# Linear attention and a two-expert MoE in one launch: gate weights loaded inside a batch's v, planned costs changed, a 96-row rest tile and new ranks

## The chip, the cores and the metric

The kernel runs on 1 core of one Trainium2 chip, in one launch. The metric is the device time in microseconds (us) of that launch.

## The reference

Linear attention over 8 batches (8 heads, 576 positions, head size 64), then a mixture of experts (MoE) on its 4608 output rows of 512:

```python
q_s = softmax(q, axis=-1)                    # over the head's 64
k_s = softmax(k, axis=2)                     # over the 576 positions
kv  = einsum('bhsd,bhse->bhde', k_s, v)
attn = einsum('bhsd,bhde->bhse', q_s, kv)
x   = attn.transpose(0, 2, 1, 3).reshape(4608, 512)
logits = x @ w_gate + modality_bias[modality_id]       # 8 experts
e = argmax(logits);  gate = softmax(logits)[e]
out[row] = gate * (relu(x[row] @ w1[e]) @ w2[e])       # w1 512x1024, w2 1024x512
```

With this draw the bias decides the expert, so all rows of modality 0 (2277 of them) go to one expert and all of modality 1 (2331) to another.

## The kernel before

**Work.** For each batch b, q, k and v come by DMA from SyncE's queue into five staging buffers `st` (two halves of a transfer for b = 0 to 2, one transfer after that). ScalarE takes the exponentials of q and k. VectorE sums q per head (`sq`, L883), and takes the reciprocal (`iq`, L894 and L895). GpSimd multiplies q by it (`nq`, L899, five steps). TensorE transposes and sorts q by modality with a permutation matrix (`s1`, L1101; the matrix is `perm`, L928, on VectorE), builds kv (`kv`, L1014), and VectorE normalizes it (`ki`, L1041 and L1044; `kb`, L1050). TensorE then multiplies the two (`s2`, L1140), and ScalarE and VectorE copy the columns to their places in `xs` (`put`, L1171): rows of modality 0 from the left ("side a"), of modality 1 from the right ("side b").

**Places.** They come from the modality ids: `isa`, `turn`, `isa2`, `rank`, `pos`, `off` and `aoff` count; `slot`, `digits`, `hhi`, `hv`, `hlo`, `id` and `idx` make the list of row numbers for the stores; `bsel` (GpSimd, L727 to L732) gives each row its bias.

**Experts.** The two experts' weights come by GpSimd's queue into `W` (`wi`, L537 and L548): a1 and a2 are w1 and w2 of side a, b1 and b2 those of side b, each in two pieces. GpSimd needs the experts' numbers for this (`eid`). The first, a1, also awaits the second half of q1. The gate weights (`lwg`, L478, four small DMAs of SyncE's queue; `wgc`, L609, their cast on VectorE) are needed by the logits. Each side works off nine passes of 256 rows: logits (L1217), `gates`, h = relu(x w1) (L1289 on TensorE; L1251 and L1253 the relu on ScalarE or VectorE), y = h w2 (L1302), scaling (L1257, L1259) and one indirect store for each 128 rows (L1262, GpSimd). The boundary between the two modalities lies within one more tile, the rest (`ffn_rest`), whose expert is chosen at run time: `copy_x`, a copy of the weights, h (L1455), y (L1468) and a store.

**Order.** Nothing of the order is written by hand. `Plan.order` simulates the kernel with assumed costs: every engine, when idle in the plan, starts the ready step with the least priority, and the order that comes out is the order of each engine's real queue, which is served strictly in order. A step's priority is its `rank` plus the first number that `TUNED` has for its key; the second number is added on VectorE and GpSimd where a step may go to more than one engine. `Plan.later` holds a step back until another is done, in the plan alone. DMA loads keep the order of `transfers`. `Plan.fill` puts matmuls that nobody reads (`unread`, L1556) into TensorE's planned idle time up to `quiet`, at which one PSUM buffer more joins the ring.

```python
self.prio = {e: rank + more + (late if ALONE[e] and len(costs) > 1 else 0.0) for e in costs}
```

After the plan a few steps test that all the assumptions on the draw hold (counts per batch, one expert for each modality); only where they don't, a slow loop at the end runs.

Of the kernel before, what the change touches and what calls it, by code (L numbers as in the profile page):

```python
# [19 lines left out]
P = 128  # L20
# [224 lines left out]
def kernel(  # L245
# [27 lines left out]
    GW = 256  # L273

    passes_a = [(n, 256 * n, 256) for n in range(B)] + [(B - 1, 256 * B, 256)]
    passes_b = [(n, N - lo - w, w) for n, lo, w in passes_a]
    W2 = KD * F
    WSZ = KD * F + KF * D
    OOB = 9000.0

    pool = ctx.enter_context(tc.tile_pool(name="all", bufs=1))
    psum = ctx.enter_context(tc.tile_pool(name="ps", bufs=1, space=bass.MemoryType.PSUM))

    def sb(shape, dtype, name):
        return pool.tile(shape, dtype, name=name)
# [94 lines left out]
    def hlo(c, n):  # L380
# [26 lines left out]
    bulk = [x for x in transfers if x != "g"]  # L407
    ahead_of = {(y[0], int(y[1:])): piece(x) for x, y in zip(bulk, bulk[1:]) if is_w(x) and not is_w(y)}
    w_awaits = {piece(x): at for x, at in awaited.items()}
    w_dmas = {}  # L410

    def behind(later, first, reason):
        tc.add_manual_dep(
            later.ins,
            first.ins.name,
            mybir.DependencyInfo(mybir.DependencyClass.Sync, mybir.DependencyReason.DATA),
            reason=reason,
        )

    def load(nm, src, b, buf, h, n):  # L420


# [12 lines left out]

        busy = P * n * NJ * Dh * 4 / 393e3
        lat = busy + 2.0
        if not b:
            more = {("q", 0): 1.2, ("q", 2): 0.25, ("k", 0): 0.7, ("v", 2): 0.1}.get((nm, h), 0.0)
            busy, lat = busy + more, lat + more  # L440
            if (nm, h) == ("v", 2) and is_w(bulk[3]):
# [7 lines left out]
    def load_one(nm, b):  # L449
        n = 2 if b < 3 else HG  # L450
        buf = Buf(r_st)
        loads[nm, b] = ([load(nm, {"q": q, "k": k, "v": v}[nm], b, buf, h, n) for h in range(0, HG, n)], buf)
# [105 lines left out]
    def load_eids(_):  # L558
# [8 lines left out]
        )  # L567

    w_issue = [pl.op({"POOL": (1.0, 1.0)}, load_eids, [o_exp], key="eid", rank=-1)]

    def landing(nm, b, h):
        ls = loads[nm, b][0]
        return ls[h // (HG // len(ls))]

# [286 lines left out]
    def attention(b):  # L861
# [341 lines left out]
        if not b:  # L1203
            pl.later(wg_c, kvbds[0])
# [509 lines left out]
```

## Time and profile before

| | |
|---|---|
| time before, median of 3 runs | 195.91 us (194.67 to 196.11) |
| the profiled execution's own time | 194.22 us |
| its span, from the first to the last instruction | 192.6 us |
| TensorE busy in the span | 178.3 us (93%) |
| of that, matmuls that nobody reads (L1556) | 13.7 us |
| VectorE, ScalarE, GpSimd busy | 143.7, 126.1, 104.8 us |

Times in rows are counted from the span's start. PE is TensorE, DVE VectorE, ACT ScalarE, POOL GpSimd, SP SyncE; a "q" behind the name is the engine's own issuing queue. "[0.40 <-POOL eq L899]" behind a row says that the engine stood idle for 0.40 us before it, until that step was done.

### The profile page before, as it was taken

Reading aid. Unit: us, or ns where it says so; the run is one execution under the profiler, and the core shown is the slowest. Engines: PE = TensorE matmul, PEld = TensorE weight load, DVE = VectorE, ACT = ScalarE, POOL = GpSimd, SP = SyncE. Lnnn points to the kernel's source line nnn. Section 1 sums busy time; section 2 is a strip of 40 time slices with the busy share of each in tenths; the row PEclk is TensorE's granted clock in tenths of the full one; section 3 lists DMA queues with packets and bytes.
Section 4 is the critical chain, followed back from the end, with each engine's and each line's share of the span. In section 5 each row is a group of like instructions: output and inputs, shape, how many; then the busy total and the mean of one; then the engine's idle time right before and its main releaser. Section 6 shows DMA issues by size and latency. Waiting matters only on the chain.

```text
span 192.6 us, 4997 instructions
## 1 busy us (share of the span) xinstructions
PE 178.3 (93%) x1750; PEld 122.9 (64%) x1750; DVE 143.7 (75%) x394; ACT 126.1 (65%) x246; POOL 104.8 (54%) x133
## 2 busy tenths in 40 slices
PE   2989888999999999999999989899999999999980
PEld 0445446585894787588667765599576767457650
DVE  5988865999999999579969949969677344436550
ACT  2788826989768779999989398498899222210000
POOL 6079959069927793981498229993240422233252
PEclk9999999999999999999999999999999999999998
DMA  5999999999999999989998920230040201114123
GB/s 184 364 401 392 252 210 210 228 396 280 200 378 374 408 411 406 394 260 380 398 396 274 386 92 2 109 114 2 3 163 3 109 13 54 50 57 157 54 109 117
DMA packets 18637, 42.34 MB, mean 220 GB/s; under 512 B 1961, under 2 KB 1961, under 8 KB 18610
## 3 DMA queue, kind: packets, MB, share of 16 engines
q1 hardware_dynamic: 13392, 28.33, 40.7%
q0 software_dynamic: 5200, 13.64, 24.6%
q8 instruction: 14, 0.23, 0.5%
q14 instruction: 13, 0.11, 0.2%
q10 hardware_dynamic: 18, 0.04, 0.1%
HBM read 36.75 MB, written 9.70 MB: 241 GB/s over the span
## 4 chain that ended last, share of the span: by engine, by line
PE 72%; DMA 13%; POOL 5%; DVE 3%; issue 3%; ACT 2%; POOLq 0%; DVEq 0%; ACTq 0%
PE ps L1289 30%; PE ps L1302 29%; DMA st<-in_q_dram 8%; DMA wg_f<-in_moe_w_gate_dram 5%; PE ps L1140 4%; POOL eq L899 3%; PE ps L1101 3%; PE ps L1014 2%; POOL out_dram L1262 2%; PE ps L1217 1%; DVE own L883 1%; PE ps L1455 1%; PE ps L1468 1%; ACT st L877 1%; PE ps L778 1%
## 5 line engine op out<-in xcount | busy, mean ns | idle before, releaser
L1289 PE MATMUL ps<-xs,W 128*128 128x256 bf16 x576 | 69.7, 273 | 1.3 <-ACT hT L1251 1.3
L1302 PE MATMUL ps<-W,hT 128*128 128x512 bf16 (+1 forms) x296 | 65.9, 373 | 0.0
L1289 PEld LDWEIGHTS <-W 128*128 128x128 bf16 x576 | 54.3, 98 | 10.0 <-issue 2.6
L1262 POOL DMA_INDIRECT out_dram<-y_sb,idx x36 | 35.8, 995 | 42.2 <-DVE y_sb L1259 19.6
L899 POOL TENSOR_TENSOR eq<-st,qi 128x512 bf16<-128x512 f32 (+1 forms) x40 | 37.9, 971 | 16.2 <-DVE qi L895 6.7
L1302 PEld LDWEIGHTS <-hT 128*128 128x128 bf16 x296 | 28.1, 98 | 28.7 <-issue 0.3
L1251 ACT ACTIVATE hT<-ps 128x512 bf16<-128x512 f32 x43 | 24.8, 601 | 19.9 <-PE ps L1302 9.0
L1259 DVE TENSOR_SCALAR y_sb<-ps,gate 128x512 f32<-128x512 f32 (+1 forms) x26 | 18.8, 721 | 21.0 <-PE ps L1302 16.2
L1171 ACT CAST xs<-ps 128x256 f32 (+1 forms) x90 | 29.2, 432 | 2.4 <-PE ps L1140 1.2
L1253 DVE TENSOR_SCALAR hT<-ps 128x512 bf16<-128x512 f32 x31 | 21.1, 684 | 4.8 <-PE ps L1289 3.2
L883 DVE TENSOR_REDUCE own<-st 128x18 f32<-128x1152 f32 x16 | 21.6, 1348 | 2.5 <-ACT st L877 2.4
L910 ACT ACTIVATE ek<-st 128x1152 bf16<-128x1152 f32 x16 | 18.8, 1174 | 5.8 <-DMA st<-in_k_dram 5.1
L877 ACT ACTIVATE st<-st 128x1152 f32<-128x1152 f32 x16 | 18.6, 1172 | 3.3 <-DMA st<-in_q_dram 3.3
L1171 DVE CAST xs<-ps 128x256 f32 (+1 forms) x54 | 20.0, 417 | 0.6
L920 POOL CAST vb<-st 128x1152 bf16<-128x1152 f32 x9 | 10.3, 1158 | 11.9 <-PE ps L1289 7.2
L1101 PE MATMUL ps<-perm,eq 128*128 128x128 bf16 x144 | 13.5, 220 | 1.5 <-POOL eq L899 0.9
L1556 PE MATMUL ps<-ones 128*128 128x512 bf16 x46 | 13.7, 434 | 1.2 <-POOL ones L339 1.2
L1101 PEld LDWEIGHTS <-eq 128*128 128x128 bf16 x144 | 9.7, 98 | 5.9 <-POOL eq L899 3.3
L1115 DVE CAST et<-ps 128x512 bf16<-128x512 f32 (+1 forms) x19 | 11.9, 626 | 1.4 <-PE ps L1101 1.3
L1113 ACT CAST et<-ps 128x512 bf16<-128x512 f32 (+1 forms) x21 | 11.1, 544 | 2.7 <-PE ps L1101 2.6
L1236 ACT ACTIVATE ex<-L,gmx 128x8 f32<-128x8 f32 x36 | 8.8, 307 | 4.2 <-DVE gmx L1232 4.2
L1140 PE MATMUL ps<-et,kvbd 128*128 128x128 bf16 (+1 forms) x160 | 11.2, 214 | 0.2 <-ACT et L1113 0.2
(137 smaller groups left out, 171.5 us busy)
## 6 DMA issues: line engine op xcount, KB each, us to landing
st<-in_q_dram SPq DMA_DIRECT2D x5, 1152.0 KB, 9.9
st<-in_k_dram SPq DMA_DIRECT2D x5, 1152.0 KB, 10.2
st<-in_v_dram SPq DMA_DIRECT2D x5, 1152.0 KB, 10.9
st<-in_q_dram SPq DMA_DIRECT2D x6, 576.0 KB, 5.6
st<-in_k_dram SPq DMA_DIRECT2D x6, 576.0 KB, 7.6
st<-in_v_dram SPq DMA_DIRECT2D x6, 576.0 KB, 10.5
W<-in_moe_w_dram POOLq DMA_DIRECT2D x8, 256.0 KB, 10.5
W<-in_moe_w_dram POOLq DMA_DIRECT2D x4, 512.0 KB, 9.4
```

Source lines behind the costliest of these rows:

```text
L877: nc.scalar.activation(out=t, in_=t, func=ACT.Exp)
L883: nc.vector.tensor_reduce(out=sums[qib.idx][:, h * NJ : (h + n) * NJ], in_=view(st[bq.idx], [[Dh, n * NJ], [1, Dh]], h * NJ * Dh), op=ALU.add,
L899: (nc.vector if e == "DVE" else nc.gpsimd).tensor_tensor(out=view(eq[eqb.idx], [[HG * Dh, n], [Dh, HG], [1, Dh]], j0 * HG * Dh), in0=view( ...
L910: nc.scalar.activation(out=view(ek[ekb.idx], [[Dh, n], [HG * Dh, NJ], [1, Dh]], h * Dh), in_=view(st[bk.idx], [[NJ * Dh, n], [Dh, NJ], [1, ...
L1101: nc.tensor.matmul(out=view(t, [[2 * nj * 64, 2], [1, 64]], hp * nj * 64 + jj * 64), lhsT=eq[eqb.idx][:, j0 + jj, P * hp : P * hp + P], rh ...
L1140: nc.tensor.matmul(out=view(ps_t[xbuf.idx], [[1, nj * 64]], c * nj * 64), lhsT=kvbd[kvb.idx][:, c, :], rhs=et[etb.idx][:, c, j0 * 64 : (j0 ...
L1171: w_ = nc.scalar.copy(out=dst, in_=src) if e == "ACT" else nc.vector.tensor_copy(out=dst, in_=src)
L1251: nc.scalar.activation(out=dst, in_=src, func=ACT.Relu)
L1253: nc.vector.tensor_scalar_max(out=dst, in0=src, scalar1=0.0)
L1262: s_ = nc.gpsimd.indirect_dma_start(out=out, out_offset=bass.IndirectOffsetOnAxis(ap=ix[:, c : c + 1], axis=0), in_=ysb, in_offset=None, b ...
L1289: m = nc.tensor.matmul(out=t[:, i * w : (i + 1) * w], lhsT=w1(W[:, slot_, :], kd, f), rhs=xs[:, kd, lo : lo + w], start=(kd == 0 and kds = ...
L1302: nc.tensor.matmul(out=t, lhsT=h[:, kf, i * P : (i + 1) * P], rhs=W[:, slot_, W2 + kf * D + c0 : W2 + kf * D + c0 + cn], start=(kf == 0), ...
```

## The change

1. The gate weights' four DMAs are issued between the two halves of batch 1's v; before, they stood behind v1 in `transfers`.
2. Planned costs alone: `slot` 1.3 to 1.55 us, `bsel` 1.8 to 2.2, each W piece of w1 1.25 to 1.3 on GpSimd; the first W piece behind a load takes 0.7 longer in the plan, and the last part of a load that stands ahead of W lands 1.2 later.
3. The rest tile's copy of x, its h matmuls and its relu are 96 columns wide and not 128; the relu is ScalarE's alone. The test of the assumptions is narrowed likewise (2277 is within 96 of 2304, so the draw still meets it).
4. Five fixed places are gone (`Plan.later`): `slot` and `bsel` behind batch 0's `nq`; the loads of offsets (`lo`) behind `nq` or `cv`; `wgc` and batch 1's `perm` behind batch 0's `kb`.
5. `quiet` is 38 and not 40 us, and all of `TUNED` is new. Of the keys that matter below, the priority (rank plus first number) before and after:

| key | before | after | key | before | after |
|---|---|---|---|---|---|
| isa2 | -6.5 | 141.5 | perm1 | -21.5 | -65 |
| sq0.2 | -9 | 1 | lo0 | -90.8 | -99.8 |
| iq0 | 72.5 | 1 | bsel | 209.5 | 13 |
| pos | -69 | 40 | slot | 521 | 79.5 |
| off | -93 | -62.5 | wgc | -180.5 | 31 |
| perm0 | -139 | -34.5 | ki0 | 28 | 26.5 |
| ekk5 | 497 | -21.5 | ekk6 | 180.5 | -104 |

```diff
-    transfers = "q0 k0 v0 q1 k1 v1 g a1 a2 b1 q2 k2 v2 b2".split()
+    transfers = "q0 k0 v0 q1 k1 v1 a1 a2 b1 q2 k2 v2 b2".split()
...
+        for h in range(0, HG, n):
+            if h and (nm, b) == ("v", 1):
+                l_wg.append(pl.op({"DMA": (0.4, 2.4)}, load_wg, key="lwg", rank=0))
+            ls.append(load(nm, {"q": q, "k": k, "v": v}[nm], b, buf, h, n))
...
+        if h + n == HG and (nm, b) in ends:
+            lat += 1.2
...
-        cost = 1.25 if part < 2 else 0.8
+        cost = 1.3 if part < 2 else 0.8
...
+        w += 0.7 if (s, part) in first_w else 0.0
...
-    o_slot = pl.op({"POOL": (1.3, 1.45, True)}, slot_run, [o_aoff], key="slot", rank=12)
+    o_slot = pl.op({"POOL": (1.55, 1.7, True)}, slot_run, [o_aoff], key="slot", rank=12)
...
-    o_bsel = pl.op({"POOL": (1.8, 2.0, True)}, bsel_run, [o_aoff, o_exp], key="bsel", rank=13)
+    o_bsel = pl.op({"POOL": (2.2, 2.4, True)}, bsel_run, [o_aoff, o_exp], key="bsel", rank=13)
...
-        if not b:
-            for o in (o_slot, o_bsel):
-                pl.later(o, nq[-1])
...
-        if not b:
-            for o in los:
-                pl.later(o, nq[-1] if "DVE" in o.costs else cv[-1])
...
-        if not b:
-            pl.later(wg_c, kvbds[0])
-        if b == 1:
-            pl.later(perms[1], kvbds[0])
...
+    RW = 96
...
-                            out=ps_t[fb.idx][:, f * P : (f + 1) * P],
+                            out=ps_t[fb.idx][:, f * RW : (f + 1) * RW],
                             lhsT=w1(wx(0), kd, 4 * i + f),
-                            rhs=xx[:, kd, :],
+                            rhs=xx[:, kd, 0:RW],
...
-    quiet = 40.0
+    quiet = 38.0
```

## Rows read from the trace of the kernel before

**Rows 1.** The page: busy time by engine, and 40 slices of the span.
```profile
PE 178.3 (93%) x1750; PEld 122.9 (64%) x1750; DVE 143.7 (75%) x394; ACT 126.1 (65%) x246; POOL 104.8 (54%) x133
...
PE   2989888999999999999999989899999999999980
```

**Rows 2.** Stretches of 8 us: busy by engine, clock, DMA share, GB/s.
```profile
24.00:32.00 8.00, 6.72 (x75) 4.18 (x73) 5.13 (x22) 3.39 (x8) 5.75 (x12) 1.00 1.12 210
...
104.00:112.00 8.00, 6.70 (x99) 5.76 (x97) 7.64 (x25) 4.97 (x9) 3.18 (x3) 1.00 0.96 355
...
120.00:128.00 8.00, 7.50 (x75) 5.43 (x74) 6.56 (x17) 5.55 (x17) 7.42 (x9) 1.00 0.28 101
```

**Rows 3.** What PE waited for from 26 us on: us, times, longest.
```profile
PE ps L1289 <- ACT hT L1251: 1.3, 1, 1.3
PE ps L1101 <- POOL eq L899: 0.9, 2, 0.5
```

**Rows 4.** PE in order of time, 24 to 48 us.
```profile
26.89 0.61 PE L1289 MATMUL ps<-xs,W 128*128 128x256 bf16 x4
...
39.06 3.65 PE L1289 MATMUL ps<-xs,W 128*128 128x256 bf16 x32
```

**Rows 5.** GpSimd in order of time, from batch 0's nq to batch 1's.
```profile
10.98 4.68 POOL L899 TENSOR_TENSOR eq<-st,qi 128x512 bf16<-128x512 f32 x5 [6.74 <-DVE qi L895]
...
17.96 2.69 POOL L537 DMA_DIRECT2D W<-in_moe_w_dram  x4
...
25.91 0.59 POOL L537 DMA_DIRECT2D W<-in_moe_w_dram  x1 [1.51 <-DMA W<-in_moe_w_dram]
...
27.50 0.35 POOL L703 TENSOR_TENSOR slot<-na,kt 128x72 f32<-128x72 f32 x1
...
29.28 4.68 POOL L899 TENSOR_TENSOR eq<-st,qi 128x512 bf16<-128x512 f32 x5
```

**Rows 6.** VectorE in order of time, batch 0's sums to its perm.
```profile
8.07 1.36 DVE L883 TENSOR_REDUCE own<-st 128x18 f32<-128x1152 f32 x1
...
9.48 0.23 DVE L667 TENSOR_SCALAR na<-ps 128x72 f32<-128x72 f32 x1
...
10.24 0.19 DVE L894 TENSOR_SCALAR qi<-own 128x36 f32<-128x36 f32 x1
...
10.76 1.29 DVE L928 TENSOR_TENSOR perm<-own,posx 128x1152 bf16<-128x1152 f32 x1
```

**Rows 7.** All in order of time: batch 0's last side-a copy, v1's end, gate weights.
```profile
23.30 0.36 ACT L1171 CAST xs<-ps 128x256 f32 x1
...
24.38 1.16 ACT L920 CAST vb<-st 128x1152 bf16<-128x1152 f32 x1 [0.71 <-DMA st<-in_v_dram]
...
25.44 0.18 DVE L609 CAST wg_sb<-wg_f 128x32 bf16<-128x32 f32 x1 [1.43 <-DMA wg_f<-in_moe_w_gate_dram]
```

**Rows 8.** SyncE's issues in order of time: v1's second half, gate weights.
```profile
11.25 0.37 SPq L424 DMA_DIRECT2D st<-in_v_dram  x1
...
14.57 2.10 SPq L478 DMA_DIRECT2D wg_f<-in_moe_w_gate_dram  x2
```

**Rows 9.** The chain that ended last: 128-wide matmuls of the rest, 64-wide ones of s2.
```profile
105.27 0.12 PE ps L1140 x4
...
145.31 0.89 PE ps L1455 x16
```

**Rows 10.** Groups by line and form: the rest's weight loads.
```profile
L1455 PEld LDWEIGHTS <-st 128*128 128x128 bf16 x32 | 2.0, 98 | 0.0
```

**Rows 11.** All engines in order of time around 110 us.
```profile
109.91 1.16 ACT L910 ACTIVATE ek<-st 128x1152 bf16<-128x1152 f32 x1 [3.02 <-DMA st<-in_k_dram]
...
111.61 1.03 PE L1289 MATMUL ps<-xs,W 128*128 128x256 bf16 x8 [1.30 <-ACT hT L1251]
```

**Rows 12.** What ScalarE waited for, the whole span: us, times, longest.
```profile
ACT ek L910 <- DMA st<-in_k_dram: 5.1, 5, 3.0
ACT st L877 <- DMA st<-in_q_dram: 3.3, 5, 1.8
```

More of the change, by code (lines that the diff above doesn't have):

```diff
@@ L405, in piece @@
         return "ab".index(x[0]), 2 * (int(x[1]) - 1)
-    bulk = [x for x in transfers if x != "g"]
-    ahead_of = {(y[0], int(y[1:])): piece(x) for x, y in zip(bulk, bulk[1:]) if is_w(x) and not is_w(y)}
+    ahead_of = {(y[0], int(y[1:])): piece(x) for x, y in zip(transfers, transfers[1:]) if is_w(x) and not is_w(y)}
     w_awaits = {piece(x): at for x, at in awaited.items()}
-    w_dmas = {}
+    ends = {(x[0], int(x[1:])) for x, y in zip(transfers, transfers[1:]) if is_w(y) and not is_w(x)}
     def behind(later, first, reason):
@@ L440, in load @@
             busy, lat = busy + more, lat + more
-            if (nm, h) == ("v", 2) and is_w(bulk[3]):
+            if (nm, h) == ("v", 2) and is_w(transfers[3]):
                 lat += 0.6
@@ L444, in load @@
             busy, lat = busy + 0.3, lat + 0.3
+        if h + n == HG and (nm, b) in ends:
+            lat += 1.2
         return pl.op({"DMA": (busy, lat)}, run, rank=0, takes=[] if h else [buf], uses=[buf])
     loads = {}
[L449 to L452, printed above, removed]
     mraw = sb([B, S, 2], I32, "mraw")
@@ L567, in load_eids @@
         )
+    first_w = {piece(y) for x, y in zip(transfers, transfers[1:]) if is_w(y) and not is_w(x)}
     w_issue = [pl.op({"POOL": (1.0, 1.0)}, load_eids, [o_exp], key="eid", rank=-1)]
@@ L594, in load_w, with load_one @@
         w = 2 * P * F * 4 / 415e3
+        w += 0.7 if (s, part) in first_w else 0.0
         return pl.op({"DMA": (w, w + 2.0)}, lambda _: None, [at], lag=0.5 if part < 2 else 1.0)
+    def load_one(nm, b):
+        n = 2 if b < 3 else HG
+        buf, ls = Buf(r_st), []
+        for h in range(0, HG, n):
+            if h and (nm, b) == ("v", 1):
+                l_wg.append(pl.op({"DMA": (0.4, 2.4)}, load_wg, key="lwg", rank=0))
+            ls.append(load(nm, {"q": q, "k": k, "v": v}[nm], b, buf, h, n))
+        loads[nm, b] = (ls, buf)
     w_in, l_wg = [[], []], []
     for x in transfers:
-        if x == "g":
-            l_wg.append(pl.op({"DMA": (0.4, 2.4)}, load_wg, key="lwg", rank=0))
-        elif is_w(x):
+        if is_w(x):
             s_, part = piece(x)
@@ L1431, in copy_x @@
             nc.scalar.copy(
-                out=xx,
+                out=xx[:, :, 0:RW],
                 in_=bass.AP(
                     tensor=xs.tensor,
-                    offset=xs.offset + (at[0] * P + (MID - P)),
-                    ap=[list(xs.ap[0]), [N, KD], [1, P]],
-                    dep_tracking_offset=xs.offset + MID - P,
+                    offset=xs.offset + (at[0] * RW + (MID - RW)),
+                    ap=[list(xs.ap[0]), [N, KD], [1, RW]],
+                    dep_tracking_offset=xs.offset + MID - RW,
                 ),
@@ L1461, in run, with relu_rest @@
                         )
+            return run
+        def relu_rest(i, fb):
+            def run(_):
+                t = hT[hb.idx]
+                o = t.offset + 4 * i * GW
+                nc.scalar.activation(
+                    out=bass.AP(
+                        tensor=t.tensor,
+                        offset=o + at[1] * (P - RW),
+                        ap=[list(t.ap[0]), [GW, 4], [1, RW]],
+                        dep_tracking_offset=o,
+                    ),
+                    in_=view(ps_t[fb.idx], [[RW, 4], [1, RW]]),
+                    func=ACT.Relu,
+                )
             return run
@@ L1488, in ffn_rest @@
         la = pl.op({"ACT": (0.6, 0.7)}, load_at, [o_mid], key="lat", rank=94)
-        xc = pl.op(on_act(KD * P), copy_x, [la, *deps], key="cx", rank=96)
+        xc = pl.op(on_act(KD * RW), copy_x, [la, *deps], key="cx", rank=96)
         wc = []
@@ L1505, in ffn_rest @@
             hm = pl.op(
-                on_pe(*[P] * (4 * KD)),
+                on_pe(*[RW] * (4 * KD)),
                 h_rest(i, fb),
@@ L1515, in ffn_rest @@
                 pl.op(
-                    {**on_act(4 * P), **on_dve(4 * P)},
-                    lambda e, i=i, fb=fb: relu(
-                        e,
-                        hT[hb.idx][:, 4 * i : 4 * i + 4, 0:P],
-                        ps_t[fb.idx].rearrange("p (f n) -> p f n", f=4),
-                    ),
+                    on_act(4 * RW),
+                    relu_rest(i, fb),
                     [hm],
@@ L1584 @@
     nc.tensor.matmul(out=n_ps[:, 0:1], lhsT=ones, rhs=cnt_b, start=True, stop=True)
-    early = sorted({(n, lo + w) for n, lo, w in passes_a if n < B - 1}) + [(B - 1, MID - P)]
+    early = sorted({(n, lo + w) for n, lo, w in passes_a if n < B - 1}) + [(B - 1, MID - RW)]
     ok = sb([1, 1 + 2 * len(early)], FP32, "ok")
```

2 lines of the change are left out of this document (1 added, 1 removed).

## The prediction

> **What bounds the kernel now.** I read the page's busy shares first [rows 1]: TensorE is busy for 178.3 us of 192.6, the other engines far less. The reader should look at the 40 slices there: TensorE's digits reach 9 in the ninth slice and stay there, with two 8s, to the end. In the first 30 us TensorE is only kept busy: 13.7 us of its total are matmuls that nobody reads. So the time is, roughly, the point at which TensorE has real work without a break, plus all real work that is left then, plus its idle time on the way, plus the tail. Of these only the first and the third can move much, since nothing here takes work from TensorE except the narrower rest tile.
>
> The idle time comes from the stretches of 8 us [rows 2]: 24 to 32 us lacks 8.00 - 6.72 = 1.28 us, 104 to 112 lacks 1.30, 120 to 128 lacks 0.50. The granted clock is 1.00 there, the full one (2.4 GHz), so no term stands for it. The waits from 26 us on name the releasers [rows 3]: 1.3 us for a relu on ScalarE, and 0.9 us in two waits for GpSimd's nq. One of these two is early, the other makes the stretch at 120 us.
>
> The start is set by the weights. The first h matmul runs at 26.89 us [rows 4], right when GpSimd's queue sees W transfers land: its ninth W issue was held until 25.91 by one of the first landing [rows 5]. GpSimd had issued the first at 17.96, when batch 0's nq (10.98 to 15.66) and bsel were over. From 39.06 on, TensorE runs on without a wait until 104 us [rows 1, 4].
>
> **The change part by part, and the sum.** The sum is made against the profiled execution's own 194.22 us, which lies 195.91 - 194.22 = 1.69 us under the median of the runs shown. I add these 1.69 us at the end.
>
> *Rest tile.* 32 h matmuls are 96 columns wide and not 128. Sixteen of 128 take 0.89 us, 55.6 ns each; four of 64 in s2, each with a weight load of its own too, take 0.12 us, 30 ns each [rows 9]. Halfway lies 42.8 ns, so 32 x 12.8 ns = 0.41 us come off TensorE, all of it on the path, since TensorE is full there. The bounds are 0, if something other than the columns sets the pace, and twice as much, if 96 ran as fast as 64. The copy of x and the relu become shorter on ScalarE; TensorE has h and y of the passes to do meanwhile, so nothing.
>
> Here the Trainium skill speaks against the edit. The weight loads of this group take 98 ns each [rows 10], more than the 55.6 ns at which the matmuls follow one another. The page "TensorE: Matmul & The Clock Gate", section "Back-to-back issue gap", says that a stream of pairs of weight load and matmul keeps about 81 ns for each matmul of 128 columns, set by both; then narrowing would give 0 and the time would be 195.1. The trace goes below that figure, with 55.6 ns at 128 and 30 ns at 64 columns under equal loads, so by these rows the loads are hidden.
>
> *Batch 0's places and nq.* The removed fixed places do less than the ranks. isa2 goes from -6.5 to 141.5, pos from -69 to 40, while iq0 goes from 72.5 to 1 and sq0.2 stands at 1. In the trace VectorE ends the second sum at 8.07 + 1.36 = 9.43 and then does pos; the reciprocal starts only at 10.24 [rows 6]. With the new ranks it comes directly behind the sum: 10.24 - 9.43 = 0.81 us earlier. nq on GpSimd waits for nothing else [rows 5], so it, bsel behind it and the first W issue move up by 0.8 us. bsel still stands ahead of W: it is ready, GpSimd has nothing else at 15 us, and the plan lets no engine stand idle. The longer planned costs of slot and bsel tell the plan what happens; they remove nothing. If W lands 0.8 us earlier, TensorE exchanges 0.8 us of matmuls that nobody reads for h.
>
> The cover for what is pushed back: off (-62.5) now goes ahead of perm0 (-34.5), so perm0 moves from 10.76 to about 12.9 (the pos block and off, about 2.1 us), and perm1 (-65), no longer held, takes another 1.3 us of VectorE before ki0 (26.5). Batch 0's last copy to side a ends at 23.66 [rows 7] and h starts at 26.89: 3.2 us of cover, 2.4 when h is 0.8 earlier. If 2.1 + 1.3 = 3.4 us all fell on that path, 1.0 us would show. But s2 also needs kv, which v0's landing sets and not perm; I take 0.
>
> *Gate weights.* VectorE was parked for 1.43 us at 25.44 until they landed, although v1's second half was in ScalarE's hands at 24.38 [rows 7]. They now land ahead of that half, and wgc goes from -180.5 to 31, behind the copies: the wait goes. What is late next is GpSimd. It issues W up to 27.5, does slot until about 29.2 and only then batch 1's nq [rows 5]; slot (79.5) still stands behind the W pieces and ahead of nq. So I count 0 for the 1.43 us themselves. The most that an earlier nq could give is TensorE's 0.9 us of waits for it [rows 3]. On SyncE's queue v1's second half moves behind four small issues. The last two ran at 14.57 to 16.67 us, so it goes from 11.25 to near 16 [rows 8]. From its old issue to its cast lie 13.1 us with all DMA engines full; the 5 us lost are covered by transfers ahead of it. If they weren't, kv and s2 of batch 1 would be later by the gap; I take 0, bounds 0 to 1.
>
> *Front together:* 0.8 us gained, between 1.0 lost (the cover above) and 0.8 + 0.9 = 1.7 gained. quiet at 38 stops the unread matmuls earlier and gives a PSUM buffer earlier, both where TensorE already has real work: 0.
>
> *From 39 us on.* All ranks are new, and the only thing there that the trace can price is TensorE's 1.30 + 0.50 = 1.8 us of idle time [rows 2]. I take it as unchanged: where the waits fall is up to the plan's errors, and the costs of the late steps are not touched. Bounds: 1.8 gained, 2.6 lost (worked out below). The tail behind the last y is the same code.
>
> Sum: 194.22 - 0.41 - 0.8 = 193.0 us; with 1.69 us for the median, **194.7 us**.
>
> **The rivals.**
>
> *A. TensorE's holes close.* The new order has neither of the two late stalls, and the front gives about what it can (1.0): 195.91 - 0.41 - 1.0 - 1.8 = 192.7. For it: both stalls come from waits behind one another in a queue, of the kind a new order moves. Against it: ten waits of ScalarE for k and q [rows 12] show that the plan's landings are too early in many places, and that isn't changed for the loads from batch 3 on.
>
> *B. ScalarE is parked on k more often; slower.* At 106.9 us ScalarE stood for 3.02 us for a k load, with a relu queued behind it, for which TensorE then lost 1.30 [rows 11]. So such a wait costs what it has over 3.02 - 1.30 = 1.7 us, and decides from there. The exponentials of k5 and k6 get far smaller priorities (497 to -21.5, 180.5 to -104): they are put into ScalarE's queue as soon as the plan believes k landed. With three waits of that length where there was one, TensorE loses 2 x 1.30 = 2.6 us more; with the rest's 0.4 and nothing from the front that is 195.91 + 2.6 - 0.4 = 198.1. Against it: of ten such waits only one cost anything.
>
> *C. The front gains nothing.* DMA is full from 24 to 32 us (share 1.12 [rows 2]), so a W that starts 0.8 us earlier takes its bandwidth from v1's second half. Then kv and s2 of batch 1 are later by as much, and TensorE, which had no idle time at 39.06, loses at the one end what it wins at the other. Left is the rest: 195.91 - 0.41 = 195.5.
>
> **How the numbers follow.** My forecast, 194.7 with a spread of about 193.5 to 196, has 0.38, A 0.23, B 0.22, C 0.17. One per cent, 1.96 us, is about what a measurement of this kernel can tell from no change: the runs shown spread by 1.4 us. Faster than 193.95 are A and the lower end of the forecast: 0.23 + 0.06 = 0.29. Slower than 197.87 are B (the greater part, 0.18) and the sums of a lost front cover and one new stall: 0.21 in all. The rest, 0.50, is within 1%. The range reaches to A's lower side and to B: 192.3 to 198.1.
>
> **What would show it.** In the new profile VectorE's reciprocal of batch 0 should start near 9.5 and not 10.24, GpSimd's nq near 10.2, the first W issue near 17.1, and the first h near 26.1. VectorE should have no wait for the gate weights, and perm0 should stand near 13. The rest's 16 matmuls should take about 0.68 us and not 0.89. For A, TensorE's busy time in all stretches from 40 to 184 us is 8.00; for B, ScalarE's waits for k have several above 1.7 us with a relu behind them; for C, W starts earlier and v1's cast moves behind 24.38 by as much. The prediction is wrong if the b0 path (perm1 ahead of ki0) delays h past 27 us, or if TensorE's idle time behind 40 us goes above 4 us.

## The result and the profile after

| | |
|---|---|
| time after, median of 22 runs | 196.55 us (194.07 to 200.75) |
| time before beside it, median of 22 runs | 194.87 us |
| ratio after to before | 1.0078 [1.0049, 1.0108] |
| forecast | 194.7 us, most likely no change |

The change made the kernel slower by 0.8%: 1.7 us more than the kernel before beside it, where the forecast was 1.2 us less. The median lies inside the range, but 1.85 us above the forecast, and the interval excludes no change. Two later comparisons of the same kernel on other chips gave 1.0022 [0.9968, 1.0076] and 1.0032 [0.999, 1.0074]: slower by less, or not at all.

The unchanged kernel was profiled three times: with the result (span 199.1 us), and as e1 (194.0) and i1 (196.1) in the experiments. The profiles with the result and of i1 are each of the slowest execution in their group (of 22 and of 12), e1's is of the third fastest of 12, so i1 shows what a bad execution holds and not the typical one. I read e1 and i1. They differ from each other as much as from the kernel before.

The stretches of 8 us of e1, which answer to [rows 2] (us, busy time and count of each engine, granted clock, DMA share, GB/s):

```profile
24.00:32.00 8.00, 6.84 (x88) 4.41 (x85) 6.33 (x22) 3.90 (x9) 5.90 (x11) 1.00 1.12 210
32.00:40.00 8.00, 7.92 (x70) 5.49 (x69) 7.71 (x19) 7.15 (x17) 1.41 (x2) 1.00 1.09 265
...
64.00:72.00 8.00, 5.88 (x82) 4.36 (x80) 5.36 (x14) 5.14 (x10) 6.46 (x7) 0.94 1.04 405
72.00:80.00 8.00, 8.00 (x66) 6.07 (x64) 7.26 (x16) 5.75 (x11) 5.72 (x6) 0.85 0.96 362
...
104.00:112.00 8.00, 8.00 (x108) 6.84 (x107) 7.58 (x25) 7.17 (x12) 5.78 (x6) 1.00 0.85 302
...
120.00:128.00 8.00, 7.83 (x91) 6.80 (x90) 6.92 (x22) 5.23 (x13) 5.71 (x7) 1.00 0.18 70
```

The two late holes (idle times of TensorE) of before, 1.30 and 0.50 us, are down to 0 and 0.17. A new hole of 8.00 - 5.88 = 2.12 us stands at 64 to 72 us, and right behind it the clock is 0.94 and 0.85: 1.2 GHz for a part of the time, which is worth (0.06 + 0.15) x 8 = 1.7 us. What TensorE waited for in e1 from 26 us on, which answers to [rows 3]:

```profile
PE ps L1017 <- issue: 2.1, 3, 1.1
PE ps L1101 <- POOL eq L905: 0.6, 1, 0.6
PE ps L1213 <- DVE xs L1171: 0.2, 1, 0.2
```

The first row is the hole, called the stop below: "issue" is a wait for nothing that the profile shows. L1017 is kv, here batch 3's. The chain that ended last in e1 (start, us, what) shows it as three gaps inside one run of 36 matmuls, none of which has a wait of its own:

```profile
67.48 0.56 PE ps L1017 x16
68.04 1.12 issue
69.17 0.21 PE ps L1017
69.38 0.50 issue
69.88 0.21 PE ps L1017
70.09 0.50 issue
70.59 0.87 PE ps L1017 x18
```

The same stretches of i1, and what TensorE waited for there:

```profile
24.00:32.00 8.00, 6.67 (x73) 3.52 (x72) 6.88 (x23) 3.62 (x8) 5.43 (x11) 0.82 1.12 211
32.00:40.00 8.00, 7.92 (x67) 5.83 (x66) 4.90 (x12) 5.03 (x12) 2.38 (x3) 0.75 1.08 267
...
72.00:80.00 8.00, 5.96 (x72) 5.00 (x68) 5.79 (x19) 4.81 (x10) 6.59 (x8) 1.00 1.04 411
```
```profile
PE ps L1017 <- issue: 2.0, 3, 1.2
PE ps L1213 <- DVE xs L1171: 1.3, 1, 1.3
```

i1 has the stop in kv too (2.04 us, this time with a full clock behind it), and a second loss at the front: a wait of 1.3 us for VectorE's copies into xs, with the clock at 0.82 and 0.75, worth (0.18 + 0.25) x 8 = 3.44 us. The wait itself is no loss against the kernel before, which lacks 1.28 us in the same stretch [rows 2], but with the clock at 1.00.

The sums against the span before (192.6 us): e1 2.12 + 1.7 for the stop, less 1.63 for the holes and 0.42 for the rest tile (below), gives +1.8, measured +1.4. For i1 it is 2.04 + 3.44 - 1.80 - 0.42 = +3.3, measured +3.5.

How much of the 0.8% each loss makes up is open. A clock loss of 3.44 us in 196.1 brings the mean clock of an execution down to about 0.983, and of the 22 executions of the result six are that low, so the front's loss as i1 has it is in six of them at most.

### The profile page after: what moved, and what is told of

The parts are those of the page before. It is cut to its first block, busy times and chain, and to the rows that moved or that the text cites. A ratio compares the mean times of both kernels' runs of the same rounds, so it can differ in the third digit from the quotient of the medians.

```text
span 199.1 us, 4962 instructions
## 1 busy us (share of the span) xinstructions
PE 181.5 (91%) x1733; PEld 125.6 (63%) x1751; DVE 146.1 (73%) x394; ACT 124.5 (63%) x246; POOL 105.1 (53%) x133
## 4 chain that ended last, share of the span: by engine, by line
PE 73%; ACT 8%; DMA 7%; DVE 5%; issue 4%; ACTq 1%; POOL 0%; DVEq 0%
PE ps L1285 29%; PE ps L1298 28%; DMA st<-in_k_dram 5%; PE ps L1017 3%; PE ps L1101 3%; PE ps L1140 3%; DMA mraw<-in_moe_modality_id_dram 2%; ACT ek L916 2%; PE ps L1566 2%; ACT xs L1171 2%; ACT st L883 2%; DVE xs L1171 1%; PE ps L1213 1%; ACT et L1113 1%; PE ps L1482 1%
## 5 line engine op out<-in xcount | busy, mean ns | idle before, releaser
L1285 PE MATMUL ps<-xs,W 128*128 128x256 bf16 x576 | 72.0, 279 | 0.0
L1298 PE MATMUL ps<-W,hT 128*128 128x512 bf16 (+1 forms) x278 | 65.0, 373 | 1.0
L1285 PEld LDWEIGHTS <-W 128*128 128x128 bf16 x576 | 55.4, 100 | 9.6 <-issue 1.5
L1255 DVE TENSOR_SCALAR y_sb<-ps,gate 128x512 f32<-128x512 f32 (+1 forms) x29 | 21.2, 729 | 19.6 <-PE ps L1298 17.9
L1247 ACT ACTIVATE hT<-ps 128x512 bf16<-128x512 f32 x35 | 20.2, 595 | 22.6 <-PE ps L1298 12.4
L1249 DVE TENSOR_SCALAR hT<-ps 128x512 bf16<-128x512 f32 x37 | 24.9, 685 | 11.3 <-PE ps L1285 9.6
L1113 ACT CAST et<-ps 128x512 bf16<-128x512 f32 (+1 forms) x30 | 16.0, 550 | 7.4 <-PE ps L1101 6.1
L926 POOL CAST vb<-st 128x1152 bf16<-128x1152 f32 x10 | 11.4, 1155 | 6.3 <-DMA st<-in_v_dram 4.1
L1017 PE MATMUL ps<-vb,ek 64*128 64x129 bf16 x288 | 11.3, 223 | 2.2 <-issue 2.1
L1140 PEld LDWEIGHTS <-kvbd 128*128 128x128 bf16 x160 | 10.3, 100 | 3.1 <-issue 0.2
```

Source lines behind the costliest of these rows:

```text
L1247: nc.scalar.activation(out=dst, in_=src, func=ACT.Relu)
L1249: nc.vector.tensor_scalar_max(out=dst, in0=src, scalar1=0.0)
L1255: nc.vector.tensor_scalar(out=dst, in0=src, scalar1=g, scalar2=None, op0=ALU.mult)
L1285: m = nc.tensor.matmul(out=t[:, i * w : (i + 1) * w], lhsT=w1(W[:, slot_, :], kd, f), rhs=xs[:, kd, lo : lo + w], start=(kd == 0 and kds = ...
L1298: nc.tensor.matmul(out=t, lhsT=h[:, kf, i * P : (i + 1) * P], rhs=W[:, slot_, W2 + kf * D + c0 : W2 + kf * D + c0 + cn], start=(kf == 0), ...
```

## The front: where i1 and e1 part

VectorE in order of time, e1 and then i1 (start, us, engine, line, operation, operands, count):

```profile
21.88 0.42 DVE L1171 CAST xs<-ps 128x256 f32 x1 [0.34 <-ACT xs L1171]
22.36 0.24 DVE L615 CAST wg_sb<-wg_f 128x32 bf16<-128x32 f32 x1
22.52 2.96 DVE L1171 CAST xs<-ps 128x256 f32 x6
```
```profile
22.96 0.42 DVE L1171 CAST xs<-ps 128x256 f32 x1 [0.34 <-ACT xs L1171]
23.30 1.24 DVE L615 CAST wg_sb<-wg_f 128x32 bf16<-128x32 f32 x1
24.46 2.95 DVE L1171 CAST xs<-ps 128x256 f32 x6
```

The cast of the gate weights (L615, 32 columns) takes 0.24 us in e1 and 1.24 us in i1, and six copies into xs are queued behind it. GpSimd's cast of v, e1 and then i1:

```profile
22.42 1.24 POOL L926 CAST vb<-st 128x1152 bf16<-128x1152 f32 x1
```
```profile
23.27 1.23 POOL L926 CAST vb<-st 128x1152 bf16<-128x1152 f32 x1
```

In e1 VectorE starts 0.06 us ahead of GpSimd; in i1 it starts 0.03 us behind, and ends at 23.30 + 1.24 = 24.54, 0.04 us behind GpSimd's end (23.27 + 1.23 = 24.50). The reader should compare the ends: in ten profiles of the change and its variants (h4 left out) the cast starts behind or inside GpSimd's, and in each of them it ends 0.04 to 0.05 us behind GpSimd's end. So it stood blocked until GpSimd was done. The Trainium skill, "SBUF — State Buffer", section "SBUF: two separate sides", says that a VectorE operation in a two-port mode and a GpSimd operation take a shared pair of ports as an exclusive lock, whichever starts first, and that an fp32 copy within SBUF is such an operation. The trace agrees, with 0.24 us for the one that comes first and 1.24 for the one that comes second.

The kernel before has this cast at 25.44 us, GpSimd's at 21.34 to 22.54, as this row of it shows: they never meet, and the cast takes 0.18 us [rows 7].

```profile
21.34 1.20 POOL L920 CAST vb<-st 128x1152 bf16<-128x1152 f32 x1
```

**An earlier meeting decides it.** At the first row shown above i1 is already 1.08 us behind e1 (22.96 against 21.88), and the blocked cast adds 1.00, so the cast is only half of the difference. The other half begins at posx (L677, the last step of `pos`, 72 columns). In the kernel before it ran ahead of nq and took 0.26 us; in the new order it runs beside nq. VectorE in e1, VectorE in i1, GpSimd in i1:

```profile
11.15 0.70 DVE L677 TENSOR_SCALAR posx<-pos,half 128x72 bf16<-128x72 f32 x1
```
```profile
11.87 1.07 DVE L677 TENSOR_SCALAR posx<-pos,half 128x72 bf16<-128x72 f32 x1
...
13.95 1.33 DVE L934 TENSOR_TENSOR perm<-own,posx 128x1152 bf16<-128x1152 f32 x1
```
```profile
15.66 0.38 POOL L733 TENSOR_SCALAR isb<-place,aoff 128x36 f32<-128x36 f32 x1 [0.74 <-ACT aoff L703]
...
17.98 2.70 POOL L534 DMA_DIRECT2D W<-in_moe_w_dram  x4
```

nq starts at 10.74 us in e1 and at 10.81 in i1, and its four steps on GpSimd take 4.11 and 4.10 us. By estimate, with four equal steps, e1's first step ends at 11.77 and i1's second at 12.86. posx ends 0.08 us behind, at 11.85 and 12.94, so it looks blocked in the same way. i1's VectorE came to posx 0.72 us later, after a wait of 0.54 us for TensorE's counts (L667), and so missed, by an estimated 0.03 us, the moment between nq's first two steps. g3 shows that this moment decides and not the 0.72 us: its VectorE reaches posx at 11.78 us, only 0.09 us before i1's, with nq begun at 10.93 and its first step over, by the same estimate, at 11.96. There posx takes 0.26 us and perm0 stands at 13.05.

The rest follows from perm0, at 13.95 us and not at 12.86. By the trace ScalarE's aoff waits for it, GpSimd's bsel, which begins with isb, waits for aoff (0.74 us), and W comes behind bsel: its first issue is at 17.98, as in the kernel before (17.96), where e1 has 17.16. Of eleven profiles with the change's order at the front (f4 and h4 left out), the four with posx at 0.70 us or less (e1, g1, g2, g3) issue W at 17.16 to 17.35; the seven with 1.06 to 1.16 us issue it at 17.98 to 18.77. These seven are the ones with the blocked cast: there both casts hang on perm0, and VectorE comes 0.03 to 0.06 us behind GpSimd each time.

What it costs on TensorE in i1, from the wait to the first h:

```profile
27.46 0.35 PE L1213 MATMUL ps<-wg_sb,xs 128*128 128x8 bf16 x8 [1.33 <-DVE xs L1171]
...
28.69 0.68 PE L1285 MATMUL ps<-xs,W 128*128 128x256 bf16 x4
```

The first h is at 28.69, in e1 at 26.94, before at 26.89 [rows 4]. Of the eleven profiles, seven have the blocked cast (1.23 to 1.25 us) and the first h at 28.69 to 29.52. Two have the cast waiting for the weights' DMA instead, as VectorE's rows of g1 and g2 show, and the first h at 28.68 and 29.35:

```profile
23.30 0.55 DVE L615 CAST wg_sb<-wg_f 128x32 bf16<-128x32 f32 x1 [0.87 <-DMA wg_f<-in_moe_w_gate_dram]
```
```profile
24.22 0.18 DVE L615 CAST wg_sb<-wg_f 128x32 bf16<-128x32 f32 x1 [1.72 <-DMA wg_f<-in_moe_w_gate_dram]
```

Two, e1 and g3, have neither, and the first h at 26.94 and 26.75. In both the clock is 1.00 from 24 to 40 us; in the other nine it falls behind the wait. The three profiles of the kernel before and its variants (before, f3, h3) have the first h at 26.89, 27.54 and 26.48.

## The experiments

I had three theories of the loss first: F (the front is late), L (the waits lie late, between batches), P (the places' steps, put behind the sums, are late). The kernels e2, e3 and e5 reorder the finished plan: `plan` is the list that `pl.order` returns, and `at(key, engine, i)` finds an entry in it. Kernels with the same letter (e to i) ran together on one chip, each letter on another one; the kernel before ran beside each.

**e1, the change unchanged, again.**

> The changed kernel as it is. The profile shown with the result had its TensorE clock at half speed in several microseconds and a stop of all engines near 73 us, so it is taken once more. Theory F (front): the loss sits ahead of 40 us, where the first h matmul now stands at 29.5 us and not 26.9; it shows here too, h between 28.5 and 29.5, and 0.5 to 1% over the kernel before. Rival L (late): the front is as late only in that one execution, and what costs time is idle TensorE behind 40 us (over 2 us in sum here).

Measured: 197.86 us median, ratio 1.0022 [0.9968, 1.0076]. The span of 194.0 us is read above.

**e2, the logits lg01 behind the second h step.**

```diff
+        o = plan.pop(at("lg01", "PE"))
+        plan.insert(at("h00", "PE", 1) + 1, o)
```

> The changed kernel with one step of TensorE's queue moved: the logits of side b's first pass, which wait for VectorE's last copy of batch 0, go behind the first two h steps of side a, as in the kernel before. Theory F: h starts 1 to 1.5 us earlier, and the time falls by 1 to 2 us, to about that of the kernel before. Rival L: no change within 0.3%. Rival P (places): the logits are only the last of a chain that is late already, since VectorE counts the places later; then the move brings less than 0.7 us.

Measured: 1.005 [1.0006, 1.0094], span 196.4. The first h came at 27.94 although the cast was blocked here too (1.24 us), 0.75 us earlier than in the earliest of the seven blocked ones. But the stop in kv was there, and nothing of the gain is left in the time.

**e3, the places' steps first on VectorE.**

```diff
+        plan.insert(at("sq0.2", "DVE"), plan.pop(at("isa2", "DVE")))
+        plan.insert(at("sq0.2", "DVE") + 1, plan.pop(at("rankr", "PE")))
+        plan.insert(at("iq0", "DVE"), plan.pop(at("pos", "DVE")))
+        plan.insert(at("off", "DVE"), plan.pop(at("perm0", "DVE")))
```

> The changed kernel with the first steps of the places in VectorE's queue put back where they were: isa2 ahead of the second sum, pos ahead of the reciprocal, perm0 ahead of off. Rival P: batch 0's s1 starts 3 us earlier (near 12.5 and not 16.1), its copies end 2 to 3 us earlier, the logits of side b no longer wait, h starts near 27, and the time falls by 1 to 2 us. Theory F with the logits alone: the copies move, but h by less than 1 us. Rival L: no change within 0.3%.

Measured: 1.0071 [1.0027, 1.0115], span 195.3. GpSimd's queue in e3 shows the price, a start of nq at 13.11 where e1 has 10.74:

```profile
13.11 4.10 POOL L905 TENSOR_TENSOR eq<-st,qi 128x512 bf16<-128x512 f32 x4 [8.89 <-DVE qi L901]
```

posx, ahead of nq here, takes 0.26 us, and so it does in e5 and g4; the first meeting is gone, but nq starts 1.9 to 2.4 us later than in e1.

**e5, both, and ScalarE's second cast of v0 ahead of its parked load of offsets.**

```diff
+        plan.insert(at("lo0", "ACT"), plan.pop(at("cv0.1", "ACT")))
```

> The changed kernel with three moves at once: the places' steps first on VectorE, v0's second cast ahead of the load of offsets on ScalarE, and side b's logits behind two h steps on TensorE. If the whole loss is in the front (F or P), this is at least as fast as the kernel before, 0 to 1% faster (the narrower rest remains, 0.4 us). Rival L: still 0.5% or more slower.

Measured: 1.0021 [0.9989, 1.0053], span 195.6. P falls in the form tested: no move of the places returns 1 us. All four profiles have the stop in batch 3's kv (2.1 us, in e2 2.3), and none has another hole of that size behind 40 us. F seemed to fall too, since e1's first h, at 26.94, is not late. The new question was whose the stop is. In every one a load of 16 KB on a DMA queue that the profile calls "instruction", and that I take for TensorE's code, starts 0.2 to 0.6 us behind the end of the stop, so theory C was: the stop belongs to the place of kv in TensorE's code. Theory S: it belongs to kv and to what runs beside it.

**f1, f2: more instructions ahead of kv.** Five (f1) or 35 (f2) of the early matmuls that nobody reads are cut in four: the same columns, but 30 or 210 rows more in TensorE's program.

```diff
+        n_unread[0] += 1
+        for i in range(4 if n_unread[0] <= 5 else 1):
+            if n_unread[0] <= 5:
+                nc.tensor.matmul(out=ps_t[n_ps - 1][:, i * P : (i + 1) * P], lhsT=ones, rhs=ones, start=True, stop=True)
```

> The change, with five of the early unread 512-wide matmuls each cut in four of 128 columns: the same columns and TensorE time, but 15 more pairs of instructions (30 rows) ahead of everything behind 26 us. In every profile of the change so far TensorE stops about 2.1 us inside batch 3's kv, at the 16th to 19th of its 36 pairs per half, in steps of 0.71 us, with no wait named. Theory C (the stop belongs to a place in TensorE's instruction stream, where its code is loaded): the stop moves 15 pairs earlier in the program, to the first pairs of kv3 or the last of the h step ahead of it, where pairs are 109 ns apart, and is shorter or gone. Theory S (the stop belongs to kv3 and to what the other engines and queues do beside it, whatever the code's place): it stays within kv3 at the same distance from its start (0.4 to 0.6 us), 2.1 us long. Time: S as the change, ratio 1.002 to 1.008; C 0.985 to 1.008.

> The change, with 35 of the early unread matmuls each cut in four of 128 columns: 105 more pairs, 210 rows, about one load of TensorE's code (256 rows) less 46, which puts the code loads against kv3 as the kernel before has them (there the fifth load comes 45 rows later in the program than in the change). Theory C: no stop in kv3; the span falls by 2 to 3.7 us against the change (the stop and the half clock behind it), ratio to the kernel before 0.982 to 0.992. Theory S: the stop stays in kv3, ratio 1.002 to 1.008.

Measured: f1 0.9996 [0.9935, 1.0057], f2 1.0104 [0.9993, 1.0215]. Neither has the stop; kv runs in 0.99 us, counted from the start of its first matmul to that of its last (with the last one itself it is 1.20). This read as C, and S seemed to fall, for the six stores beside kv lie as before. But f2 was not faster. Its stretches show the front instead, with a wait of 1.3 us for xs:

```profile
24.00:32.00 8.00, 6.73 (x76) 3.73 (x75) 6.96 (x23) 3.70 (x8) 5.42 (x11) 0.86 1.13 212
32.00:40.00 8.00, 7.87 (x64) 5.79 (x63) 4.72 (x12) 4.88 (x11) 2.46 (x3) 0.71 1.06 262
```

**f3, the kernel before with 48 rows more**, by the same edit with eight.

> The kernel before, with eight of its early unread matmuls each cut in four of 128 columns: 24 more pairs, 48 rows, which puts its kv3 against the code loads where the change has it. Theory C: a stop of about 2 us appears in kv3 of the kernel before (its own kv3 runs through in 0.99 us), ratio 1.008 to 1.02. Theory S: kv3 stays at 0.99 us, ratio 0.997 to 1.003.

Measured: 1.0036 [0.996, 1.0112], kv 0.98 us: no stop. The half of C that said the stop could be brought into the kernel before was not borne out.

**f4 and h4, kv of batch 3 behind two more h steps**, in h4 with its two readers on VectorE.

```diff
+        for name, eng in (("kv3", "PE"), ("ki3", "DVE"), ("kb3", "DVE")):
+            plan.insert(at("h20", "PE", 1), plan.pop(at(name, eng)))
```

> The change, with batch 3's kv moved behind two more h steps (28 pairs, about 2 us) in TensorE's order. Theory C: the pairs at which TensorE stopped are now those of the h steps, which need their instructions a quarter as fast: kv3 runs in 0.99 us, and a stop of up to 2 us shows in the h steps or not at all. Theory S with the six output stores of GpSimd as the neighbour (in all five profiles the stop begins 0.45 to 0.51 us behind the start of the fifth store and ends 0.95 to 1.09 us behind the end of the sixth): kv3 now starts about when the sixth store ends, so at most one step of 0.71 us is left. Theory S with kv3's own operands: the stop moves with kv3, 2.1 us long. Time: without the stop 0.985 to 0.995 of the kernel before, with it 1.002 to 1.008.

> The change with batch 3's kv and its two readers on VectorE (the reciprocal and the block of K times V) moved behind two more h steps and a first product: kv3 starts 56 rows later, at row 1233, and the rows at which it stopped (1209 to 1219) hold pairs of 64 and 256 columns. Theory C: kv3 runs in 0.99 us; at the old rows TensorE may stop up to 2.1 us or not, as pairs of 109 ns ask for code less fast. A theory by kv3's own operands: the stop moves with it, kv3 3.1 us or more.

Measured: 3370 us, and 198.47 us in one execution. In f4 kv stands behind its own readers, so batch 3's product of K and V is a wrong one and the kernel ran its general path; h4 computes a wrong product too. In h4 kv took 0.99 us, but so did the kv of every kernel beside it. Neither tells anything.

**g1, g2: 6 and 12 rows more**, one and two cut.

> The change with one early unread matmul cut in four: 3 more pairs, 6 rows ahead of kv3. With 30 rows and with 210 rows more, kv3 ran in 0.99 us beside the same six stores, so the stop goes with where TensorE's code lies. Theory C-broad (the stop comes whenever kv3's pairs stand ahead of the fifth load of code within some tens of rows): with 6 rows it is still there, 2.1 us, starting about 6 rows earlier within kv3. Theory C-sharp (an exact alignment of a few instructions): it is gone, kv3 0.99 us, time as with 30 rows.

> As the run with 6 rows, with two unread matmuls cut: 12 rows. C-broad: the stop is there, 12 rows earlier within kv3 or a step of 0.71 us shorter. C-sharp: gone, kv3 0.99 us.

Measured: 196.88 and 197.67 us, one execution each; kv 0.99 and 0.98 us, no stop. By C the place would have to be sharp.

**g3, f1's kernel again, and g4, with e5's three moves.**

> The kernel with 30 rows again, for its time: its three undisturbed runs at a clock over 0.99 had spans of 190.8 to 192.0 us, the kernel before 190.6 to 194.4 (mean 192.7), the change 192.4 to 195.1. Theory C: ratio to the kernel before 0.990 to 0.997, so the rest of the change gains 0.6 to 1.8 us and the stop was what made it slower. If the stop costs nothing in timed runs: 1.002 to 1.008, as the change.

> 30 rows more, with the three moves of the front at once (steps of places ahead on VectorE, ScalarE's cast ahead of its parked load, logits behind the second h step). With the stop these moves gave 1.0021 against 1.0022 for the change alone, so they are worth about nothing; with 30 rows alone the logits matmul waits 1.3 us at 26.4 us, which the third move takes away. Expected: no stop in kv3, ratio 0.987 to 0.995; if the wait at 26 us is only put off, as with 30 rows alone.

Measured: g3 0.996 [0.9928, 0.9992], median 192.71 us; g4 1.0008 [0.9979, 1.0036], 193.86 us. g3's profile has neither loss, and is the shortest of all, 190.3 us, where f1's, of the same kernel, has the late front and 196.3 us. g3's stretches and its waits from 26 us on:

```profile
24.00:32.00 8.00, 6.92 (x92) 4.48 (x91) 6.33 (x22) 3.93 (x9) 5.87 (x11) 1.00 1.12 211
32.00:40.00 8.00, 7.87 (x70) 5.50 (x69) 7.71 (x19) 7.14 (x17) 1.43 (x2) 1.00 1.06 268
```
```profile
PE ps L1101 <- POOL eq L905: 1.0, 2, 0.8
PE ps L1101 <- DVE hT L1249: 0.3, 1, 0.3
```

The three moves cost g4 0.5% against g3; nq is at 12.67 us there.

**h1, h2, h3: 2 rows more, 6 rows more at the end, and 2 rows more in the kernel before.** h1 and h3 cut the first unread matmul in two; h2 adds three pairs behind everything, where kv keeps its place in the code.

```diff
+    for i in range(3):
+        nc.tensor.matmul(out=ps_t[1][:, i * P : (i + 1) * P], lhsT=ones, rhs=ones, start=True, stop=True)
```

> The change with its first unread matmul cut in two: one more pair, 2 rows ahead of kv3. With 6, 12, 30 and 210 rows more the stop in kv3 is gone. Theory C (place of kv3 in TensorE's code): with 2 rows either still there (2.1 us, by 2 rows earlier in kv3) or gone, which gives the width of the place. Theory D (anything of the program as a whole, its length or where its code lies in memory): any outcome.

> The change with three unread pairs (6 rows) added at the end of TensorE's work, behind the last h and y steps: the program is as long as the one with 6 rows ahead, but kv3 keeps its place in the code. Theory C: the stop stays, 2.1 us inside kv3. Theory D: it is gone, kv3 0.99 us.

> The kernel before with its first unread matmul cut in two: its kv3 then starts at row 1177, the row at which the change has it. Theory C with the place counted from the start of the program: a stop of about 2 us in kv3 of the kernel before. If kv3 still takes 0.99 us, the row alone does not make the stop; how far ahead of TensorE its sequencer stands there, which differs between the two kernels, must come in too.

Measured, one execution each: 196.46, 195.99 and 195.8 us, no stop in any, kv 0.98 to 0.99 us. I took h2 for the end of C, since its kv has the place of the change's. Left were the program as a whole (D here, P in the next two expectations), and a possibility that I had overlooked (H): all kernels of one letter share a chip, and the unchanged kernel had not been run beside f, g and h.

**i1 and i2: the unchanged kernel and h2's, on one chip.**

> The change unchanged, on the chip of the next kernel. So far every profile of the change and of its re-orderings with the same number of instructions has the stop of 2.1 us in batch 3's kv (five profiles in two calls), and every profile with instructions added has none (six profiles in three other calls), so chip and program are not yet apart. Theory P (the program as a whole makes the stop: its length, where its code lies): the stop is there, ratio 1.002 to 1.010. Theory H (the chip or the call makes it): no stop here, kv 0.99 us, ratio 0.992 to 0.999.

> The change with three unread pairs behind all its other matmuls, so that nothing stands otherwise ahead of or around batch 3's kv. Theory P: no stop, kv 0.99 us, ratio 0.990 to 0.999, and 1 to 2.5 us faster than the change beside it at the same clock. Theory H: as the change beside it within 0.5 us, stop or no stop.

Measured: i1 1.0032 [0.999, 1.0074], i2 1.0034 [0.9988, 1.0081]. Both have the stop. TensorE in h2 and then in i2, the same kernel on two chips:

```profile
71.57 1.20 PE L1017 MATMUL ps<-vb,ek 64*128 64x129 bf16 x36
```
```profile
71.69 0.63 PE L1017 MATMUL ps<-vb,ek 64*128 64x129 bf16 x16
72.71 0.21 PE L1017 MATMUL ps<-vb,ek 64*128 64x129 bf16 x1 [0.40 <-issue]
73.44 0.21 PE L1017 MATMUL ps<-vb,ek 64*128 64x129 bf16 x1 [0.51 <-issue]
74.85 0.69 PE L1017 MATMUL ps<-vb,ek 64*128 64x129 bf16 x18 [1.20 <-issue]
```

So the program as a whole falls as well: the same kernel has the stop on one chip and not on another. Of the change and its variants, all seven profiles with the result, of e and of i have the stop, and none of the nine of f, g and h (f4 left out). The stop goes with the chip, or with the time at which the letter ran. What makes it there is open. kv's place in the code does not make it alone, since h2 has the change's place and no stop. But a part of C is not excluded: instructions were added ahead of kv only on chips without a stop, so nobody knows whether they would remove it where it occurs, and f3 and h3 do not speak against C either. Open too is whether the kernel before has the stop: its three profiles (before, f3, h3) show none, but none of them was taken beside e or i.

The kernels with the change's order at the front by what their profiles show, spans in us (g1 and g2 are late by the wait for the weights' DMA):

| | no stop in kv | stop in kv |
|---|---|---|
| first h by 26.94 | g3 190.3 | e1 194.0 |
| first h at 28.68 or later | h2 194.4, f2 194.5, h1 194.9, g1 195.2, g2 196.1, f1 196.3 | i1 196.1, i2 196.7, with the result 199.1 |

So theory F came back, with causes that I had not thought of, and a part of P with it, since posx is one of the places' steps. By this table the late front costs 194.4 - 190.3 = 4.1 us or more without the stop and some 2 with it. Most of it is the clock: in h2 it is 0.85 and 0.72 from 24 to 40 us, worth (0.15 + 0.28) x 8 = 3.4 us. The stop costs 3.7 with a good front, since the clock falls behind it in e1, and about 1.7 with a late one in i1, where it doesn't. These are differences between single executions on several chips, so each is good to about 1 us.

The timed executions point at the stop as well. At a mean clock of 0.99 or more there is no room for the front's 3.4 us. There the change has mean spans of 194.0 us (e1, three executions) and 193.3 (i1, six), the kernel before beside it 193.2 and 193.3; the kernel of f1 and g3, on chips where no profile has the stop, has 191.4 (f1, three) and 190.9 (g3, eight), the kernel before beside it 192.2 and 192.4. So the change's order is 0.0 to 0.8 us behind on the first two chips and 0.8 to 1.5 us ahead on the other two. The difference fits the 2 us of the stop, but chip and kernel change together, and the unchanged kernel has not run where the stop is absent.

## Why the prediction was wrong

The term that failed is "Front together: 0.8 us gained", in two of its steps. Neither asked what VectorE and GpSimd do at the same moment.

*Batch 0's places and nq.* "nq on GpSimd waits for nothing else, so it, bsel behind it and the first W issue move up by 0.8 us", and the pos block and off take "about 2.1 us". bsel also waits for aoff, which now comes behind perm0, and pos, moved behind the reciprocal, runs beside nq. In seven of eleven profiles posx took 1.06 to 1.16 us and not 0.26, perm0 stood at 13.95 us or later (forecast 12.9), bsel waited 0.74 or 0.75 us for aoff, and W was issued at 17.98 us or later: none of the 0.8 us was left.

*The gate weights.* "The wait goes" and "I count 0". The 1.43 us wait for the DMA did go in most profiles. But wgc did not land behind the copies, as the step put it: six of VectorE's copies of batch 0 stand behind it in the new order. So what delays this cast delays them, then the logits on TensorE, which stand ahead of kv and the first h. And the cast, moved 1 to 3 us forward, now falls on GpSimd's cast of v and takes 1.23 to 1.25 us in the same seven profiles.

In place of the 0.8 us gained the runs showed a first h about 2 us late in nine of eleven profiles, past the 27 us that the prediction gave as a sign of being wrong, and a clock between 0.60 and 0.91 behind it, from 24 to 40 us; in i1 that is 3.44 us lost, in e1 the front gained 0. This is seen in the profiles, by executions that fell on either side of the two meetings; no run moved posx or the cast alone, so the gain from undoing them is not measured.

*From 39 us on.* "I take it as unchanged" failed both ways. The 1.8 us of holes did close, as rival A had it: e1 lacks 0.17 us there. The stop in kv took their place, 2.0 to 2.3 us in the seven profiles with the result, of e and of i. The prediction has no term for it. No row of before shows it, and whether it belongs to the change or to the chip is open.

*The range.* 196.55 us lies within 192.3 to 198.1 only because the range reaches up to B's price. B's mechanism did not occur, so that is luck.

*The front without the blocked cast.* GpSimd issued the first W at 17.16 us in e1 (forecast 17.1, before 17.96), yet only 0.24 us of this came from the sum. VectorE's and GpSimd's rows of e1:

```profile
8.61 1.34 DVE L889 TENSOR_REDUCE own<-st 128x18 f32<-128x1152 f32 x1
9.88 0.21 DVE L659 CAST isa<-ps 64x72 bf16<-64x72 f32 x1
10.02 0.17 DVE L900 TENSOR_SCALAR qi<-own 128x36 f32<-128x36 f32 x1
...
12.86 1.33 DVE L934 TENSOR_TENSOR perm<-own,posx 128x1152 bf16<-128x1152 f32 x1
```
```profile
10.74 4.11 POOL L905 TENSOR_TENSOR eq<-st,qi 128x512 bf16<-128x512 f32 x4 [6.47 <-DVE own L672]
...
17.16 2.70 POOL L534 DMA_DIRECT2D W<-in_moe_w_dram  x4
```

The second sum itself started 0.54 us later (8.61 against 8.07 [rows 6]), behind the steps that choose the experts, and isa2 came between it and the reciprocal. So the reciprocal was at 10.02, not 9.5, and nq at 10.74, not 10.2. The rest came from the last of nq's five blocks, which VectorE took: 4.11 us on GpSimd and not 4.68. The first h did not follow: 26.94 for a forecast of 26.1. W was there earlier, but on TensorE the logits and kv of batch 1 stood ahead of h. The 0.8 us gained is therefore 0, which is rival C's result by another way. perm0 at 12.86 (forecast 12.9) cost nothing visible here, as taken. v1's second half was issued at 16.62 (near 16), as this row of SyncE's queue shows, and its cast came at 24.80, 0.42 us later than before:

```profile
16.62 0.37 SPq L424 DMA_DIRECT2D st<-in_v_dram  x1
```

*The rest tile* was right: the chain of e1 has

```profile
175.68 0.68 PE ps L1451 x16
```

for a forecast of 0.68, 42.5 ns for each matmul, so 32 x 13.1 ns = 0.42 us came off. The Trainium skill's figure of about 81 ns for a pair of weight load and matmul ("TensorE: Matmul & The Clock Gate", "Back-to-back issue gap") does not hold in this group: it is given for 128 columns, where the rows have 55.6 ns [rows 9], and 96 take 42.5.

*The rivals.* A's mechanism came true from 80 us on, and with a good front and no stop most of its size too: g3's span is 2.3 us under the one before, for 195.91 - 192.7 = 3.2 forecast; its ratio is 0.996. B fell: ScalarE has no wait for k among its longest in e1, where it had 5.1 us in five waits [rows 12]. What made the kernel slower was none of the three.

One reading of the prediction is off without weight: TensorE's digits [rows 1] reach 9 for good in the eighth slice, not the ninth.

## What to carry to other kernels

Before a short VectorE operation is moved, look at what GpSimd does at that moment in its new place, and at what is queued behind it: 72 columns took 1.07 us and not 0.26, 32 columns 1.24 and not 0.24, and the wait of TensorE at the end of the queue (1.33 us) was followed by 3.44 us of lost clock. When two executions of one kernel part, follow both back to the first row at which they differ: here that was more than 10 us ahead of the wait that it led to. When an experiment removes a stall, run the unchanged kernel on the same chip before the edit gets the credit; several variants here were credited wrongly until that was done. One profile of a kernel with a close race is one of its outcomes: e1 alone would have hidden the front, and i1 alone would have made too much of it.

## What the hardware showed unexpectedly

A VectorE operation of 72 or 32 columns took 1.07 or 1.24 us beside a GpSimd operation and ended 0.08 us (by estimate) or 0.04 us behind it, where it takes 0.26 and 0.18 us alone. TensorE stopped inside a run of matmuls without waits, for 2.0 to 2.3 us, its single matmuls between the gaps about 0.7 us apart, on one chip and not on another with the same kernel. Behind a stop or a wait of 1.3 us the granted clock fell to 1.2 GHz for some of the next microseconds in many profiles (0.60 to 0.91 in stretches of 8 us behind the front's wait, 0.94 and 0.85 in e1), but not behind the stops of e3, i1 and i2 and not behind the 1.30 us of the kernel before; what tells these apart is not shown. The kernel before had mean spans between 192.2 and 193.3 us at a clock of 0.99 and above, by chip (four chips), the higher ones on the two chips with the stop.
